# Short convolution and SwiGLU feed-forward on one core: block 2 transposed by DMA, unit 1's x loaded late and copied inside SBUF, casts in shorter rows

## The chip, the cores and the metric

The kernel runs on one core of one Trainium2 chip. The metric is the device time of one execution in microseconds. The kernel before takes 775.95 us (median of 3 runs, 775.26 to 776.23).

## The reference

The input x has 8 sequences of 4096 tokens with 192 channels in float32; the output has the same shape. The reference computes a causal convolution along the tokens and then a gated feed-forward layer:

```
w = softmax(weight, axis=-1)                     # 8 heads, 7 taps
conv[b, s, ch] = sum_k w[head(ch), k] * x[b, s - 6 + k, ch]     # 24 channels a head, zeros before the sequence
g = conv @ w_gate;  val = conv @ w_val           # 192 -> 1536
out = (g * sigmoid(g) * val) @ w_out             # 1536 -> 192
```

## The kernel before

The 32768 tokens are 64 blocks of 512 tokens, and four blocks are a unit: 16 units. The loop at L899 runs over 768 steps, 12 a block, one for each 128 columns of the hidden layer. In step n `gate_val(n)` (L771) makes six 64-row weight loads with matmuls of 64x512 (gate and val on the two halves of the array), ScalarE takes the SiLU of the gate, and VectorE multiplies it with val. Every third step a `slot` (L839) adds 24 matmuls of 64x192 of the down projection. Step 24 is the first of block 2, step 36 of block 3 and step 48 of unit 1.

For a block, `gate_val` needs the convolved tokens with the channels on the partitions: three tiles `xc[b][0..2]` of 128x512. They are made in three ways.

- Blocks 0 to 3 (unit 0) go through `early` (L373): TensorE multiplies x, loaded as overlapping windows (`xe`), with a band matrix; ScalarE and VectorE move the result into `tme`, which still has the tokens on the partitions. Blocks 0, 1 and 2 are then turned by `eturn` (L437): 15 TensorE transposes of 128x128 into three PSUM banks, and three copies on VectorE and ScalarE. Block 3 is turned by `eout` (L416), two stores of `tme` into a DRAM scratch `scre`, and `efetch` (L426), three DMA transposes from it. `early(2)` is issued inside the slot of step 12, `eturn(2)` in step 18, `early(3)` inside the slot of step 19, `eout(3)` and `efetch(3)` in steps 20 and 21.
- Units 1 and 3 go through `conv_half` (L460), which multiplies the tile `x16[u]` with the band matrix `band`: 32 matmuls each, inside the slots of steps 25 and 31 for unit 1. `x16[u]` holds the windows of x twice, in partitions 0 to 31 and 32 to 63 (and 64 to 95 and 96 to 127 for the second half of the windows). For unit 1 `load_x` (L129) reads all four pieces from DRAM, 480 KB each, before the loop starts. For unit 3 it reads two of them during unit 1, after a named SiLU, and `dup_x` (L144) copies them to the other partitions with two DMAs of 480 KB inside SBUF. The results are stored (`conv_out`, L506) and fetched by DMA transposes (`fetch`, L528).
- Units 2 and 4 to 15 are "pooled": `cast_x` (L576) casts the unit's x from DRAM into a float16 DRAM scratch `xs`, DMA transposes fetch it, and VectorE, ScalarE and GpSimd do the convolution. The cast of unit 2 is issued in step 21.

The function `seq` (L73) fixes the order of the instructions of each engine as they are written. So GpSimd's queue holds its loads and casts in program order, and SyncE (SP)'s queue holds every store, transposing fetch and copy in program order; an instruction that waits holds all that stand behind it on that engine. In the order before, SP's queue around the change is: the output of block 0 (step 17, L867), `eout(3)`, `efetch(3)`, the small fill for the cast (L583), the output of block 1, the stores of unit 1. GpSimd's is: windows `xe`, weights, `xe` again, the four loads of `x16[1]`, the four copies that build `band` (L364), the cast of unit 2 (L590).

Of the kernel before, what the change touches and what calls it, by code (L numbers as in the profile page):

```python
# [10 lines left out]
def kernel(  # L11
# [61 lines left out]
    def seq(i):  # L73

        e = i.ins.engine
        if e in last_on:
            tc.add_manual_dep(i.ins, last_on[e].name, NOSYNC, reason="order")
        last_on[e] = i.ins
        return i
# [15 lines left out]
    def windows(t, p0, t0, size, w0, w1, i0=0, i1=None, at=0, after=None):  # L95
        i1 = i1 or (Q if size == EO else size + pad)
        i = seq(
            nc.gpsimd.dma_start(  # L98
                out=t[p0 + i0 : p0 + i1, w0 - at : w1 - at, :],
                in_=bass.AP(  # L100
                    tensor=x_flat.tensor,
                    offset=(t0 + size * w0 - pad + i0) * D,
                    ap=[[D, i1 - i0], [size * D, w1 - w0], [1, D]],
                ),
            )
        )
        if after is not None:
            tc.add_manual_dep(i.ins, after.name, SYNC, reason="load in turn")
# [17 lines left out]
    def x16_tile(u):  # L126
        x16[u] = cpool.tile([P, 4 * NG, D], fp16, tag="x16", name="x16")

    def load_x(u, r, after=None, low=0):  # L129
        t, t0, w0, p0 = x16[u], u * UT, 4 * NG * r, Q * r + low  # L130
        w1 = w0 + 4 * NG
        if r == 0 and u % upb == 0:
            seq(nc.gpsimd.memset(t[0:pad, 0, :], 0.0))
            windows(t, p0, t0, CO, 0, 1, i0=pad, after=after)
            windows(t, p0, t0, CO, 1, w1)
        elif r == 1 and u == NU - 1:
            last = (UT - 1) // CO
            seq(nc.gpsimd.memset(t[p0 : p0 + 32, last - w0 :, :], 0.0))
            windows(t, p0, t0, CO, w0, last, at=w0)
            windows(t, p0, t0, CO, last, last + 1, i1=UT - CO * last + pad, at=w0)  # L140
        else:
            windows(t, p0, t0, CO, w0, w1, at=w0, after=after)

    def dup_x(u, queue=None):  # L144
        for r in range(2):
            p0 = Q * r
            seq(
                (queue or nc.sync).dma_start(
                    out=x16[u][p0 + 32 : p0 + 64], in_=x16[u][p0 : p0 + 32]
                )  # L150
            )
# [69 lines left out]
    xe_tile(3)  # L221
    xe_load(3)
    x16_tile(1)
    for r in range(2):
        for low in (0, 32):
            load_x(1, r, low=low)

    pq_i = small("pq_i", [P, 1], i32)
    seq(nc.vector.tensor_single_scalar(pq_i, pid, 15, op=ALU.bitwise_and))
# [186 lines left out]
    def eout(e):  # L416
        scre[e] = dpool.tile([XW, 4 * Q], fp16, tag="scre", name="scre")
        rows = scre[e].rearrange("(g c j) d -> c j g d", c=2, j=EO)
        for c in range(2):
            seq(  # L420
                nc.sync.dma_start(
                    out=rows[c], in_=tme[e][Q * c : Q * c + EO, :, :]
                )
            )

    def efetch(b):  # L426
        xc[b] = []
        for k in range(SL):
            t = cpool.tile([P, XW], fp16, tag=f"xc{k}", name=f"xc{k}", bufs=6)
            seq(  # L430
                nc.sync.dma_start_transpose(
                    out=t[:, 0:TB], in_=scre[b][0:TB, Q * k : Q * k + P]
                )
            )
            xc[b].append(t)

    def eturn(b, where):  # L437
        xc[b] = []
        for k in range(SL):
            t = cpool.tile([P, XW], fp16, tag=f"xc{k}", name=f"xc{k}", bufs=6)  # L440
            pool, tag = where[k]
            bank = pool.tile([P, EG, P], fp16, tag=tag, name="turn")
            for g in range(EG):
                seq(
                    nc.tensor.transpose(  # L445
                        bank[:, g, :], tme[b][:, g, Q * k : Q * k + P], ident
                    )
                )
            seq(
                (dve, act, dve)[k](  # L450
                    t.rearrange("p (g c j) -> p g c j", c=2, j=EO),
                    bank.rearrange("p g (c q) -> p g c q", c=2)[:, :, :, 0:EO],
                )
            )
            xc[b].append(t)
# [47 lines left out]
    def conv_dup(u):  # L503
        seq(nc.gpsimd.tensor_copy(tm[u][:, :, SL * Q : 4 * Q], tm[u][:, :, 0:Q]))  # L504
# [45 lines left out]
    def make_picks():  # L550
        for name in which:
            pick[name] = small(f"pick_{name}", [H, P], fp16)
            seq(
                nc.vector.scalar_tensor_tensor(
                    pick[name], which[name], float(grp), above[name],
                    op0=ALU.is_lt, op1=ALU.mult,
                )
            )
# [17 lines left out]
    def cast_x(u):  # L576
        rows = XP + UT
        xs[u] = dpool.tile([rows, D], fp16, tag="xs", name="xs")
        flat = xs[u].rearrange("t d -> (t d)")
        skip = XP if u % upb == 0 else 0  # L580
        if skip:
            seq(
                nc.sync.dma_start(  # L583
                    out=flat[0 : XP * D].rearrange("(a n) -> a n", n=P),
                    in_=fill[0 : XP * D // P, :],
                )
            )
        n = (rows - skip) * D // P
        seq(
            nc.gpsimd.dma_start(  # L590
                out=flat[skip * D : rows * D].rearrange("(a n) -> a n", n=n),
                in_=bass.AP(
                    tensor=x_flat.tensor,
                    offset=(u * UT - XP + skip) * D,
                    ap=[[n, P], [1, n]],
                ),
            )
        )
# [109 lines left out]
    def pooled(u):  # L708
        return u in POOLED
# [59 lines left out]
    silu = {}  # L769
# [117 lines left out]
    gate_bank, val_bank = (ppool, "gate"), (ppool, "val")  # L887
    acc_banks = (apool, "acc0"), (apool, "acc1")
# [10 lines left out]
    for n in range(n_steps):  # L899
        b, j = divmod(n, NCH)  # L900
        u, ls = divmod(n, ustep)
        work = None
        if n in (12, 19):

            def work(e=2 if n == 12 else 3):
                early(e, (gate_bank, gate_bank, val_bank))

        at = (25, 31) if u == 0 else (10, 22)
        if u + 1 < NU and not pooled(u + 1) and ls in at:

            def work(u=u, hh=at.index(ls)):
                conv_half(u + 1, hh)

        gate_val(n)
        if n == 6:
            early(1, (*acc_banks, gate_bank))
        elif n == 8:
            eturn(1, (*acc_banks, gate_bank))
        elif n in (9, 12, 15, 17):
            k = {9: 1, 12: 2, 15: 3, 17: 4}[n]  # L920
            slot(k, 0, silu[n - 1 if k == 4 else n - 2], work)
        elif j % 3 == 1 and n > 18:
            if j == 4 and act_steps and act_steps[0][0] < (
                dve_steps[0][0] if dve_steps else n_jobs[0]
            ) + 3:
                act_steps.pop(0)[1]()
            k = {1: 3, 4: 4, 7: 1, 10: 2}[j]
            slot(k, b - 1 if j < 7 else b, silu[n - 2], work)
        if n == 18:
            eturn(2, (*acc_banks, gate_bank))  # L930
        elif n == 20:
            eout(3)
        elif n == 21:
            efetch(3)
        if n == 34:
            make_picks()
        if n == 37:
            make_channel_taps()
        pooled_work(n, j, work is not None)
        if u + 1 < NU and not pooled(u + 1):  # L940
            if ls == at[0]:
                conv_dup(u + 1)
            if ls == at[1]:
                for m in range(2):
                    conv_out(u + 1, m)
            if ls == at[1] + 1:
                for m in range(2, 8):
                    conv_out(u + 1, m)
            lo = 32 if u == 0 else 28
            if ls in range(lo, lo + 12, 3):  # L950
                fetch(UB * (u + 1) + (ls - lo) // 3)
        if u + 2 < NU and not pooled(u + 2):
            if ls == (21 if u == 0 else 1):
                x16_tile(u + 2)
                load_x(u + 2, 0, silu[n - 1])
            if ls == (23 if u == 0 else 5):
                load_x(u + 2, 1, silu[n - 1])
            if ls == (37 if u == 0 else 26):
                dup_x(u + 2)
        for job in plan.pop(n, ()):  # L960
            job()
# [42 lines left out]
```

## Time and profile before

| | before |
|---|---|
| median of 3 runs | 775.95 us (775.26 to 776.23) |
| the profiled execution | 775.12 us, span 773.3 us |
| TensorE (PE) busy | 766.8 us, 99% |
| weight loads (PEld) / VectorE / ScalarE / GpSimd busy | 645.5 / 688.9 / 636.8 / 578.8 us |
| DMA moved | 79.32 MB, mean 103 GB/s |
| DMA queue q1 (issued from SP) | 61.58 MB, 36.3% of 16 engines |
| DMA queue q0 (issued from GpSimd) | 15.96 MB, 13.3% of 16 engines |

Times are microseconds from the start of the span of one profiled execution, which is 1.8 us shorter than that execution's own time. A row of the timeline reads: start, length, engine, line, operation, what it writes <- what it reads, shape, how many; in brackets the idle time of that engine before it and what ended that. SPq is the queue of SyncE, whose rows show how long it took to issue DMAs, not how long the data took. In the table of stages the DMA share can be over the stage's length where packets overlap.

### The profile page before, as it was taken

To read this page: it belongs to the slowest core of one execution; us is meant where nothing else is said; L and a number is where in the kernel's file an instruction comes from. 1 tells how busy PE (TensorE), PEld (TensorE's weight loads), DVE (VectorE), ACT (ScalarE), POOL (GpSimd) and SP (SyncE) were. 2 spreads that over 40 slices of the span, in tenths; PEclk is the share of its full clock that TensorE was granted. 3 is DMA by queue.
4 is the path that set the end of the run, shared out by engine and by line. 5 is a ranking of instruction groups with operands and counts; after the bars stand their busy time and mean duration, and the time that the engine had idled before them with its cause. 6 is when DMAs were issued, how large, how long until landed. Compare 5 with 4: busy or idle time off the path is not lost.

```text
span 773.3 us, 27884 instructions
## 1 busy us (share of the span) xinstructions
PE 766.8 (99%) x11179; PEld 645.5 (83%) x11179; DVE 688.9 (89%) x1034; ACT 636.8 (82%) x1093; POOL 578.8 (75%) x525
## 2 busy tenths in 40 slices
PE   8999999999999999999999999999999999999997
PEld 5666686668888888888888888888888888888886
DVE  7677998899999999999999999999999999997775
ACT  6667888888888888888888888888888888886664
POOL 8100796799989999898989989999899998882000
PEclk9999999999999999999999999999999999999999
DMA  9959855854635436355363543627454352221211
GB/s 134 190 125 135 169 118 108 158 105 101 115 96 113 107 86 106 89 118 115 77 119 84 109 101 80 123 78 122 88 111 111 87 121 74 56 70 39 67 57 42
DMA packets 143652, 79.32 MB, mean 103 GB/s; under 512 B 89146, under 2 KB 143042, under 8 KB 143042
## 3 DMA queue, kind: packets, MB, share of 16 engines
q1 hardware_dynamic: 130690, 61.58, 36.3%
q0 software_dynamic: 12832, 15.96, 13.3%
q8 instruction: 87, 1.43, 0.8%
q14 instruction: 43, 0.35, 0.2%
HBM read 31.92 MB, written 37.83 MB: 90 GB/s over the span
## 4 chain that ended last, share of the span: by engine, by line
PE 99%; ACT 0%; DVE 0%; issue 0%
PE gate L780 47%; PE acc L806 33%; PE val L780 18%; PE warm L880 0%; PE turn L445 0%; PE cv L476 0%; PE cv L387 0%; PE acc L827 0%; ACT tme L405 0%; ACT wide L345 0%; ACT o_sb L972 0%; PE taps L332 0%; DVE spread L312 0%; PE ctap L565 0%; DVE tap L310 0%
## 5 line engine op out<-in xcount | busy, mean ns | idle before, releaser
L791 DVE TENSOR_TENSOR h<-sig,val 128x512 f16<-128x512 f16 x768 | 498.8, 684 | 75.3 <-PE gate L780 51.8
L789 ACT ACTIVATE sig<-gate 128x512 f16<-128x512 f32 x768 | 458.2, 597 | 120.1 <-PE gate L780 71.8
L780 PE MATMUL gate<-pxc,w 64*128 64x512 f16 x1872 | 437.7, 376 | 0.0
L780 PE MATMUL val<-pxc,w 64*128 64x512 f16 x1872 | 437.6, 376 | 0.0
L780 PEld LDWEIGHTS <-w 64*128 64x128 f16 x4608 | 366.1, 110 | 85.2 <-issue 0.9
L806 PEld LDWEIGHTS <-h 64*128 64x128 f16 x6096 | 286.8, 94 | 29.4 <-issue 1.4
L806 PE MATMUL acc<-wo,h 64*128 64x192 f16 x6096 | 308.5, 243 | 0.0
L632 POOL TENSOR_TENSOR total<-total,part 128x512 f32<-128x512 f32 x156 | 198.3, 1271 | 64.7 <-DVE total L657 47.4
L657 DVE SCALAR_TENSOR_TENSOR total<-x,both_taps,total 128x512 f32<-128x512 f16 x156 | 166.0, 1064 | 0.0
L647 POOL TENSOR_SCALAR piece<-x,both_taps 128x512 f32<-128x512 f16 x156 | 142.9, 916 | 0.0
L632 POOL TENSOR_TENSOR total<-total,piece 128x512 f32<-128x512 f32 x78 | 111.1, 1424 | 6.5
L682 ACT ACTIVATE part<-x,both_taps 128x512 f32<-128x512 f16 x156 | 111.5, 715 | 0.0
L780 PE MATMUL val<-xc,w 64*128 64x512 f16 x432 | 102.0, 376 | 0.0
L780 PE MATMUL gate<-xc,w 64*128 64x512 f16 x432 | 101.9, 376 | 0.0
L632 POOL TENSOR_TENSOR pxc<-total,piece 128x512 f16<-128x512 f32 x52 | 66.8, 1285 | 4.3
L682 ACT ACTIVATE total<-x,both_taps 128x512 f32<-128x512 f16 x78 | 55.8, 716 | 0.0
L632 POOL TENSOR_TENSOR y<-total,piece 128x512 f16<-128x512 f32 x26 | 33.1, 1274 | 2.2
L864 DVE COPY o_sb<-acc 128x384 f32<-128x384 f32 x63 | 34.6, 549 | 0.0
L863 ACT COPY o_sb<-acc 128x384 f32<-128x384 f32 x63 | 29.8, 473 | 4.5 <-PE acc L806 4.5
L98 POOL DMA_DIRECT2D x<-in_x_dram x6 | 5.1, 871 | 24.4 <-ACT sig L789 24.4
L504 POOL COPY tm<-tm 128x1280 f16<-128x1280 f16 x2 | 2.5, 1252 | 17.3 <-DVE tm L493 17.3
L590 POOL DMA_DIRECT2D xs<-in_x_dram x13 | 7.2, 557 | 0.0
(67 smaller groups left out, 74.3 us busy)
## 6 DMA issues: line engine op xcount, KB each, us to landing
out_dram<-o_sb SPq DMA_DIRECT2D x63, 384.0 KB
pxc<-pxc SPq DMA_DIRECT2D x104, 64.0 KB
pxc<-y SPq DMA_DIRECT2D x104, 64.0 KB
xs<-in_x_dram POOLq DMA_DIRECT2D x7, 768.0 KB, 7.1
xs<-in_x_dram POOLq DMA_DIRECT2D x6, 774.0 KB, 6.8
x<-in_x_dram POOLq DMA_DIRECT2D x6, 480.0 KB, 10.1
scr<-tm SPq DMA_DIRECT2D x14, 130.0 KB
x<-x SPq DMA_DIRECT2D x26, 66.0 KB
```

The source lines that it names most:

```text
L98: nc.gpsimd.dma_start(out=t[p0 + i0 : p0 + i1, w0 - at : w1 - at, :], in_=bass.AP(tensor=x_flat.tensor, offset=(t0 + size * w0 - pad + i0) ...
L590: nc.gpsimd.dma_start(out=flat[skip * D : rows * D].rearrange("(a n) -> a n", n=n), in_=bass.AP(tensor=x_flat.tensor, offset=(u * UT - XP ...
L632: nc.gpsimd.tensor_tensor(job["dst"] if k == K - 1 else total, total, part, op=ALU.add)
L647: nc.gpsimd.tensor_scalar(part, shifted(k), scalar1=job["tap"][:, k : k + 1], scalar2=1.0, op0=ALU.mult, op1=ALU.mult,)
L657: nc.vector.scalar_tensor_tensor(job["total"], shifted(k), job["tap"][:, k : k + 1], job["total"], op0=ALU.mult, op1=ALU.add,)
L682: nc.scalar.activation(part, shifted(k), AF.Copy, scale=job["tap"][:, k : k + 1])
L780: nc.tensor.matmul(o, w16[m][p0 : p0 + Q, k, e::E], xc[b][k][p0 : p0 + Q, 0:TB], start=(k == 0), stop=(k == SL - 1),)
L789: silu[n] = seq(nc.scalar.activation(sg, g, AF.Silu)).ins
L791: seq(nc.vector.tensor_tensor(hj, sg, v, op=ALU.mult))
L806: nc.tensor.matmul(acc[b][bank][:, s, :], hj[p0 : p0 + Q, ts(2 * bank + s, P)], wo16[p0 : p0 + Q, j, :], start=(not second and j == 0 and ...
L863: seq(nc.scalar.copy(o_sb[:, 0:2, :], acc[b][0]))
L864: seq(nc.vector.tensor_copy(o_sb[:, 2:4, :], acc[b][1]))
```

## The change

Block 2 goes through `eout` and `efetch`, as block 3 does, in steps 13 and 14 in place of `eturn` in step 18. The four loads of `x16[1]` ahead of the loop are gone; two of them are issued in step 13, after the SiLU of step 12, and `dup_x(1)` in step 18 makes the other two pieces by copies inside SBUF, on SP's queue. All casts of x get a cap of 8192 bytes on a row, which is 2048 float32 elements.

```
@@ -221,9 +221,6 @@
     xe_tile(3)
     xe_load(3)
     x16_tile(1)
-    for r in range(2):
-        for low in (0, 32):
-            load_x(1, r, low=low)
 
     pq_i = small("pq_i", [P, 1], i32)
@@ -589,6 +586,7 @@
         seq(
             nc.gpsimd.dma_start(
                 out=flat[skip * D : rows * D].rearrange("(a n) -> a n", n=n),
+                max_dma_last_dim=8192,
                 in_=bass.AP(
@@ -926,8 +924,14 @@
             slot(k, b - 1 if j < 7 else b, silu[n - 2], work)
-        if n == 18:
-            eturn(2, (*acc_banks, gate_bank))
+        if n == 13:
+            eout(2)
+            for r in range(2):
+                load_x(1, r, after=silu[n - 1])
+        elif n == 14:
+            efetch(2)
+        elif n == 18:
+            dup_x(1)
         elif n == 20:
             eout(3)
```

## The prediction

> **What bounds the kernel now.** I read the page first, then the chain of waits, then the timelines of TensorE, VectorE, GpSimd and SP up to 60 us, where every edit but the cap on the casts lies.
>
> The page's first part and its chain, by engine:
>
> ```profile
> PE 766.8 (99%) x11179; PEld 645.5 (83%) x11179; DVE 688.9 (89%) x1034; ACT 636.8 (82%) x1093; POOL 578.8 (75%) x525
> PE 99%; ACT 0%; DVE 0%; issue 0%
> ```
>
> TensorE is the bound from end to end. Between 9 us and its last matmul, at 768.9, the trace has no two matmul starts more than 0.41 us apart. So work taken from TensorE's queue shortens the kernel one for one, a wait put into it lengthens it one for one, and what becomes faster elsewhere (the casts) gains nothing. The timeline of TensorE around the change:
>
> ```profile
> 28.45 0.38 PE L780 MATMUL gate<-xc,w 64*128 64x512 f16 x1
> 28.77 1.01 PE L445 MATMUL turn<-ident,tme 128*128 128x128 f16 x15
> 29.71 0.40 PE L780 MATMUL gate<-xc,w 64*128 64x512 f16 x1
> ...
> 37.20 0.66 PE L806 MATMUL acc<-wo,h 64*128 64x192 f16 x12
> 37.79 0.73 PE L476 MATMUL cv<-x,band 64*32 64x240 f16 x32
> ```
>
> The first three rows are the transposes of block 2 in step 18, the last the first use of `x16[1]` in step 25. The six gate and val matmuls of a step start in three pairs 0.215 apart; step 23's first pair stands at 35.26, so block 2 is first read, in step 24, at 35.91.
>
> Then VectorE's copy that completes `tme[2]`, GpSimd's queue and SP's queue:
>
> ```profile
> 23.33 0.26 DVE L414 COPY tme<-tme 128x320 f16<-128x320 f16 x1 [0.52 <-DVE tme L405]
> ```
> ```profile
> 17.40 3.42 POOL L98 DMA_DIRECT2D x<-in_x_dram  x4
> 20.78 1.76 POOL L364 COPY band<-wide 32x256 f16<-32x256 f16 x4
> 22.50 0.54 POOL L590 DMA_DIRECT2D xs<-in_x_dram  x1
> ```
> ```profile
> 28.90 0.42 SPq L867 DMA_DIRECT2D out_dram<-o_sb  x1
> 32.98 2.50 SPq L421 DMA_DIRECT2D scre<-tme  x2
> 39.08 3.83 SPq L431 DMA_TRANSPOSE xc<-scre  x3
> ```
>
> The four loads of x are issued by 20.82, and the last has landed 15.6 later, at 35.5: only 2.3 us before its first reader. Block 3's store needs 6.1 us from its first issue (32.98) until SP may issue the transposes (39.08).
>
> **What the change removes: about 1.0 us.** Without `eturn(2)`, step 19 starts one pair spacing after the pair at 28.45, at 28.67 instead of 29.71: 1.04 us. Its three evictions leave engines that wait for TensorE there, and count nothing. The two loads and the earlier DMA traffic that go away were hidden before (no stall), so they count nothing either.
>
> **What it adds: two new deadlines.** Block 2 must be in place by 35.91 - 1.04 = 34.9, and all four pieces of `x16[1]` by 37.79 - 1.04 = 36.75. Each microsecond by which the later piece misses is lost. I follow SP's queue in its new order: store of block 2, its transposes, output of block 0, two copies, store of block 3.
>
> Store: it can start when the copy at 23.33 ends, 23.6. Until its landing I have 6.1 us (block 3's, beside a cast) above; below, the stores of unit 1, issued each 0.65 us after the last with landing marks 2.1 us after issue, give 2.5. Now two x loads run beside it, so I take 5.0: 28.6.
>
> Transposes: issued in 3.83 as block 3's were: 32.4. The last lands 1.4 (undisturbed) to 2.7 after: 34 to 35, about at the deadline. A stall here is covered by the larger one below.
>
> x loads: the SiLU of step 12 starts them at 21.6, issued 0.9 apart. The nearest rows are unit 3's two loads, the first alone and the second beside transposes:
>
> ```profile
> x<-in_x_dram POOLq DMA_DIRECT2D x1, 480.0 KB, 7.6
> x<-in_x_dram POOLq DMA_DIRECT2D x1, 480.0 KB, 9.9
> ```
>
> So they land at about 29.2 and 32.4, before SP is ready to copy. Ahead of the copies stands also the output of block 0, 0.42 to issue: 32.8. The cast of unit 2 now follows the loads on GpSimd at 23.4, 0.9 later than before; its own reader waits until step 36, so that costs nothing.
>
> Copies: unit 3's are the only row, behind two outputs:
>
> ```profile
> 86.47 2.14 SPq L867 DMA_DIRECT2D out_dram<-o_sb  x2
> 88.70 1.88 SPq L148 DMA_DIRECT2D x<-x  x2
> ```
>
> The last landing mark of the second copy stands at 97.1, 8.4 after 88.70; the packets themselves run from 91.2 to 94.9. From 32.8 this gives 41.2. Below: with nothing ahead in the ring some 6 us, 38.8. Above: the cast of unit 2 is then in flight. What a cast does to SP's DMAs is seen at 143.7, where one (8.5 us to landing) runs beside eight transposes, which undisturbed take 1.25 each to issue:
>
> ```profile
> 141.85 14.83 SPq L534 DMA_TRANSPOSE xc<-scr  x8
> ```
>
> That is 4.8 us lost to one cast, whose packets (24,576 bytes, some 2 us each in the trace) alternate with short ones. Shorter rows should let SP's packets through oftener, so I add 1 us of the possible 0 to 4.8: 42.3.
>
> **The sum.** The convolution half starts at 42.3 instead of 37.79: +4.5, which already holds the -1.04. Everything behind it shifts alike. The store of block 3 comes out of SP's queue near 35 and lands behind the copies, near 43; its transposes end near 48, while step 36 is then past 50, so this adds nothing. Its cover gone, it would cost at most what the copies cost. The profiled execution, 775.12, becomes 779.6; it stands 0.83 below the median of 775.95, so the median becomes 780.4. Ends of the unknowns: store 2.5 to 6.1, copies 6 to 8.4, cast 0 to 4.8, which gives 36.3 to 47.2, net -1.04 (nothing stalls) to +9.4.
>
> **A rule against the trace.** Unit 3's loads of 480 KB took 7.6 and 9.9 us to land. The Trainium skill, "DMA: Bandwidth & Descriptors", section "Anatomy of one DMA", has a fit of 2.0 us plus the bytes over 436 GB/s, which makes such a load 3.1 us. An estimate of the whole chain by it (store 2.6, both copies 4.3) ends near 36, in time, and the median would be 774.9; the rows of this case are two to three times longer, so I keep them.
>
> A second rule speaks against the change. After the last matmul at 768.9, the granted clock in the table of stages falls to a mean of 0.75 in the last 1.2 us, after some 3.7 us of idleness. "TensorE: Matmul & The Clock Gate", section "Part 1: The HAM clock gate", says that an idle window of about 3.4 us halves the clock until some 3.4 us of work have passed. An estimate by it adds 1.7 us where one stall is that long.
>
> **The rivals.**
>
> 1. *SP's DMAs are not held and all arrive in time, or nearly.* Store 2.5, transposes 3.83 and no disturbance put the copies at 30.3, and 6 us later is 36.3, before 36.75. Then only the 1.04 is left: 774.9. For it: TensorE's own gain is certain, and the initial backlog of loads is gone by 21.6. Against: the output issued at 28.90 beside the x loads has no packet in the trace until 32.5. Anything up to 39.3 ends within 0.2% of before, which is 1.55 us and about what a measurement of this kernel can tell from no change. Chance 0.22. This is the side that is not slower; the deciding point is a landing of the second copy before 36.75.
> 2. *The store of block 2 is held until the loads and the cast are through.* They are queued back to back on GpSimd, 480 + 480 KB at the 190 GB/s of the stages at 24 to 30 us (5.2 us) and the cast (some 5 us): from 24 to 34 or 35. Then transposes end near 39, block 2 stalls step 24 by 5 us, and the copies land near 47: +9, about 785, and a lower clock could come on top. For it: the silent output at 28.90. Against: transposes at 66 to 68 us went through beside an x load, slowly. Chance 0.13.
> 3. *The cap does not change the packets,* or changes them without helping SP. Then the hold of the cast is up to 4.8 instead of my 1: +8.3 at most, within the range. It decides only where a cast meets a copy or a transpose that TensorE awaits, which happens once, near 32 to 38 us.
>
> A gain beyond 1.55 us has no row: TensorE has no other gap to close. I leave 0.03 for what I do not see.
>
> **How the numbers follow.** Late copies, net +1.6 to +8, 0.62; held store, 0.13; in time or nearly, 0.22; a larger gain, 0.03. So faster 0.03, same 0.22, slower 0.75. The late-copies case alone runs from 777.5 to 784; the range takes in the case of no stall, 774.9, and the lower part of the held store, up to 785.
>
> **What would show it.** Right: no `turn` row at 28.8; step 19 about 1 us earlier; an idle gap of TensorE of some 4 to 6 us in all between 34.9 and 43, most of it before the first `cv<-x,band` row of line 476, released by a DMA of `x<-x`; the copies issued at 32 to 35 on SP; from step 31 on the same spacing as before, shifted. Cast packets near 4 KB. Wrong: matmuls running through step 25 without a gap; or the larger gap at step 24, before the first matmul that reads block 2, which would mean that store and transposes, and not the copies, set the loss; or any gap after 60 us, which I have not priced.

## The result and the profile after

The changed kernel takes 786.56 us (median of 5 runs, 786.03 to 788.72), the kernel before beside it 775.87: 1.0145 times as long (95% interval 1.0134 to 1.0156), 10.7 us more. The profiled execution took 786.03, its span 783.8, against 775.12 and 773.3.

The page of the changed kernel, busy times and the chain by engine:

```profile
PE 769.4 (98%) x11164; PEld 681.7 (87%) x11164; DVE 688.5 (88%) x1032; ACT 635.3 (81%) x1092; POOL 577.3 (74%) x523
PE 96%; DMA 2%; SPq 1%; ACT 0%; issue 0%; DVE 0%
```

TensorE has 15 matmuls fewer, the transposes, and yet the chain that ended last now runs for 3% through transfers and through SP's queue, where 99% of it was TensorE before. The waits of TensorE between 30 and 60 us (what waited, for what: us in total, times, longest) and its timeline there:

```profile
PE gate L778 <- DMA xc<-scre: 4.9, 3, 3.2
PE cv L473 <- DMA x<-x: 3.4, 2, 2.0
```
```profile
34.85 0.38 PE L778 MATMUL gate<-xc,w 64*128 64x512 f16 x1
...
38.46 0.40 PE L778 MATMUL gate<-xc,w 64*128 64x512 f16 x1 [3.22 <-DMA xc<-scre]
...
39.94 0.42 PE L778 MATMUL gate<-xc,w 64*128 64x512 f16 x1 [1.08 <-DMA xc<-scre]
...
41.06 0.58 PE L778 MATMUL gate<-xc,w 64*128 64x512 f16 x1 [0.63 <-DMA xc<-scre]
...
45.18 0.26 PE L473 MATMUL cv<-x,band 64*32 64x240 f16 x1 [1.37 <-DMA x<-x]
47.44 1.00 PE L473 MATMUL cv<-x,band 64*32 64x240 f16 x31 [2.00 <-DMA x<-x]
```

Step 24 waits three times, once for each of block 2's transposes, and step 25 twice, once for each copy. SP's queue shows why all five are late:

```profile
24.14 1.19 SPq L418 DMA_DIRECT2D scre<-tme  x2
35.87 3.83 SPq L428 DMA_TRANSPOSE xc<-scre  x3
39.80 0.54 SPq L865 DMA_DIRECT2D out_dram<-o_sb  x1
40.39 1.27 SPq L148 DMA_DIRECT2D x<-x  x2
```

The store of block 2 is issued at 24.14, and SP may go on only at 35.87: 11.7 us. The two x loads (issued 22.28 and 23.15) have landed by 28.8 and 32.2 and the cast (24.00) by 36.0, by their landing marks, the semaphore updates that the trace records for a transfer (up to 16). The DMA view of the stage from 24 to 28 us, in which both halves of the store are issued (24.14 and 24.55), has no packet of q1, SP's queue:

```profile
q0 software_dynamic: 1493, 0.57, 131.4%
...
xs<-in_x_dram POOLq DMA_DIRECT2D x1, 768.0 KB, 12.0
x<-in_x_dram POOLq DMA_DIRECT2D x1, 480.0 KB, 9.1
scre<-tme SPq DMA_DIRECT2D x2, 130.0 KB
```

The store's first data packet comes at 28.2, 4.0 us after its issue. From there on its packets of 512 bytes alternate with those of the second load and then with the cast's of 4096 bytes, which take 0.32 us each; one landing mark after another comes in until 35.8.

A third loss stands in the table of stages (stage, then busy time and instructions of each engine, granted clock, DMA share, GB/s):

```profile
40.10:43.50 3.40, 2.77 (x20) 1.47 (x19) 0.69 (x1) 1.14 (x2) 0.00 (x0) 0.51 1.18 285
43.50:47.00 3.50, 0.57 (x7) 0.14 (x3) 0.69 (x1) 0.06 (x1) 0.00 (x0) 0.99 0.69 175
47.00:50.40 3.40, 2.96 (x49) 1.89 (x51) 1.22 (x2) 1.02 (x2) 0.90 (x1) 0.50 0.37 86
```

After each of the two stretches of waiting the clock is halved for 3.4 us. The first time this costs nothing, since the copies are awaited afterwards anyway. The second time it delays real work.

Following the first matmul of a step in both traces gives the whole account, as after minus before: step 18 +0.42 (this execution started that much later), step 19 -0.62, step 20 -0.84, step 24 +2.55, step 25 +4.89, step 26 +10.35, step 28 +10.89, and from there to step 767 it stays at +10.88. So the missing transposes won 1.26 by step 20, and the waits and the clock took 11.72 behind it. Nothing behind 51 us is won or lost.

### The profile page after: what moved, and what is told of

It is laid out like the page before. It is cut to its first block, busy times and chain, and to the rows that moved or that the text cites. A ratio compares the mean times of both kernels' runs of the same rounds, so it can differ in the third digit from the quotient of the medians.

```text
span 783.8 us, 27860 instructions
## 1 busy us (share of the span) xinstructions
PE 769.4 (98%) x11164; PEld 681.7 (87%) x11164; DVE 688.5 (88%) x1032; ACT 635.3 (81%) x1092; POOL 577.3 (74%) x523
## 4 chain that ended last, share of the span: by engine, by line
PE 96%; DMA 2%; SPq 1%; ACT 0%; issue 0%; DVE 0%
PE gate L778 38%; PE acc L804 31%; PE val L778 26%; DMA scre<-tme 1%; DMA x<-x 1%; PE warm L878 1%; SPq L428 0%; PE cv L473 0%; PE acc L825 0%; PE turn L442 0%; PE cv L384 0%; ACT tme L402 0%; SPq L148 0%; ACT wide L342 0%; ACT sig L787 0%
## 5 line engine op out<-in xcount | busy, mean ns | idle before, releaser
L778 PEld LDWEIGHTS <-w 64*128 64x128 f16 x4608 | 400.1, 110 | 64.1 <-issue 4.4
L804 PEld LDWEIGHTS <-h 64*128 64x128 f16 x6096 | 296.5, 94 | 22.2 <-issue 1.5
L804 PE MATMUL acc<-wo,h 64*128 64x192 f16 x6096 | 315.2, 243 | 0.0
L778 PE MATMUL gate<-xc,w 64*128 64x512 f16 x432 | 103.6, 380 | 5.0 <-DMA xc<-scre 4.9
L778 PE MATMUL val<-xc,w 64*128 64x512 f16 x432 | 103.8, 380 | 0.0
L630 POOL TENSOR_TENSOR y<-total,piece 128x512 f16<-128x512 f32 x26 | 33.1, 1274 | 2.2
L98 POOL DMA_DIRECT2D x<-in_x_dram x4 | 3.4, 857 | 29.2 <-ACT sig L787 29.2
L490 ACT CAST tm<-cv 128x480 f16<-128x480 f32 x8 | 4.1, 562 | 5.4 <-PE cv L473 5.4
```

The source lines that it names most:

```text
L490: eng(tm[u][:, NG * r : NG * r + NG, 2 * grp * hp : 2 * grp * hp + 2 * grp].rearrange("p g (t e) -> p g t e", t=2), banks[r][:, 0 : 2 * w] ...
L630: nc.gpsimd.tensor_tensor(job["dst"] if k == K - 1 else total, total, part, op=ALU.add)
L778: nc.tensor.matmul(o, w16[m][p0 : p0 + Q, k, e::E], xc[b][k][p0 : p0 + Q, 0:TB], start=(k == 0), stop=(k == SL - 1),)
L804: nc.tensor.matmul(acc[b][bank][:, s, :], hj[p0 : p0 + Q, ts(2 * bank + s, P)], wo16[p0 : p0 + Q, j, :], start=(not second and j == 0 and ...
```

## The experiments

Theory A: whatever SP issues while GpSimd's loads or cast have data in flight is held until these are nearly through; two transfers that TensorE needs (block 2, then the copies) queue up behind that one hold. Rivals: B, the store is slow by itself; C, only the loads hold, not the cast; D, only the loads of step 13 do the harm.

**The cast of unit 2 later** (changed kernel):

```
-            cast, jobs = 21, 55
+            cast, jobs = 30, 55      # and: the cast waits for the SiLU of its step
```

> The changed kernel, with the cast of unit 2 asked for in step 30 instead of 21, after the SiLU of that step; all else as changed. Theory A (SP's store of block 2 is held as long as GpSimd's queue has data in flight, loads and cast alike): the second store lands soon after the second x load (32.2 in the changed kernel), at 32.5 to 33.5 instead of 35.8; the transposes are issued near 33 instead of 35.87, the copies land near 44.4 instead of 47.3, and the median falls by some 3 us, to about 783.5. Rival B (the store is slow by itself, its 512-byte rows take some 11 us to DRAM): nothing moves, 786.5. Rival C (only the x loads hold it, the cast in short rows lets it through): nothing moves either, the second store still lands near 35.8.

Measured: 783.19, 7.7 over the kernel before (ratio 1.0099, 1.0084 to 1.0114). SP's queue:

```profile
24.36 1.10 SPq L418 DMA_DIRECT2D scre<-tme  x2
33.12 3.82 SPq L428 DMA_TRANSPOSE xc<-scre  x3
```

The store now takes 8.8 us instead of 11.7, and its last mark, 33.1, follows 15 of the 16 marks of the second load (by 32.6; the last stands at 34.3). So the cast made some 3 us of the hold. C falls.

**Without the cap** (changed kernel less the line `max_dma_last_dim=8192`):

> The changed kernel without the cap on the casts' rows (packets of 24,576 bytes again). Theory A: the hold lasts as long as the cast's data, whose sum of bytes is the same; the second store lands with the end of the cast, at 36 to 38 instead of 35.8, so the median is 786.5 to 789. If shorter rows let SP's packets through in earnest, the store now lands more than 3 us later and the median is over 789.5. Rival B: no change, 786.5.

Measured: 787.05 (ratio 1.0154, 1.0138 to 1.0170), and SP's transposes are issued at 35.82. With the cap the packets of the cast are 4096 bytes, without it 24,576; the hold is the same. The cap does what it says, but helps neither SP's queue here nor, alone (below), anything else.

**The x loads later** (changed kernel; loads from step 13 to step 18, cast to step 30, so that GpSimd's queue is silent while block 2 is turned):

```
-            for r in range(2):
-                load_x(1, r, after=silu[n - 1])
...
         elif n == 18:
+            for r in range(2):
+                load_x(1, r, after=silu[n])
+        elif n == 19:
             dup_x(1)
```

> The changed kernel with the two x loads asked for in step 18 after its SiLU, the copies queued behind the output of block 0 as before, and the cast in step 30, so that GpSimd's queue is silent while block 2 is stored and transposed. Theory A: the second store lands within 3.5 us of its first issue, by 27.7; the transposes are issued from there and block 2 is in place before 34.9, so that step 24 starts without a stall (the row that waits for xc<-scre disappears). The x loads then land near 36 and 38.5, the copies near 45 to 47, and one stall before the first convolution half takes all the loss: 784 to 788. Rival B: the store lands at 35 or later as in the changed kernel and step 24 stalls as there.

Measured: 784.98 (ratio 1.0129, 1.0112 to 1.0146). SP's queue and all that TensorE waited for from 30 to 60 us:

```profile
23.59 1.04 SPq L418 DMA_DIRECT2D scre<-tme  x2
26.42 3.85 SPq L428 DMA_TRANSPOSE xc<-scre  x3
```
```profile
PE cv L473 <- DMA x<-x: 8.9, 2, 6.4
```

This is the decisive run. The same store needs 2.8 us, a quarter of 11.7, block 2's last mark stands at 33.4, and step 24 does not wait. B falls. The output of block 0, issued at 30.37 beside the new place of the loads, is now the one that is held: its landing marks come from 38 to 40. The copies land at 45.7, so TensorE waits for them alone.

**The three parts alone** (each put into the kernel before):

> The kernel before with the cap on the casts' rows alone. TensorE waits for none of SP's transfers after 60 us in either kernel: no change, within 0.2% of before. If some wait of TensorE hid in the casts, it would be faster by over 0.2%.

> The kernel before with block 2 turned by store and transposes in steps 13 and 14, alone; the four x loads stand ahead of the loop and the cast in step 21 as before. Theory A (held): GpSimd's queue has data in flight from 17 to 39 us, so the store issued at 23.6 lands at 36 to 39, block 2 is in place at 41 to 44 and step 24 stalls by 6 to 9 us: 781 to 785, more with a halved clock. Rival D (only the loads asked for in step 13 do the harm, by meeting the store): the store lands near 28.6, block 2 by 34.9, and the removed 1.04 us shows: 774.5.

> The kernel before with the two late x loads of step 13 and the copies of step 18, alone; block 2 is turned on TensorE in step 18 as before, the casts have no cap. Theory A: the second load lands near 32.2, the copies are issued then, behind the output of block 0, which the loads and the cast hold until some 36; the copies land at 40 to 42 instead of the 37.8 at which they are needed: net +2 to +5, 778 to 781. If the copies alone made the loss of the whole change, 786; if they are hidden, 775.5.

The cap alone: 775.30 (ratio 0.9996, 0.9987 to 1.0005), no change. Block 2 alone: 781.20 (1.0075, 1.0061 to 1.0088), +5.5. The late loads and copies alone: 777.40 (1.0024, 1.0015 to 1.0033), +1.7. The sum of the parts is 7.1, the whole 10.7. SP's queue with block 2 alone, then with the late x alone:

```profile
24.30 0.81 SPq L421 DMA_DIRECT2D scre<-tme  x2
31.90 7.71 SPq L431 DMA_TRANSPOSE xc<-scre  x3
```
```profile
28.90 0.42 SPq L864 DMA_DIRECT2D out_dram<-o_sb  x1
29.38 5.13 SPq L148 DMA_DIRECT2D x<-x  x2
```

What TensorE waited for from 30 to 60 us with block 2 alone:

```profile
PE gate L780 <- DMA xc<-scre: 4.8, 3, 3.6
```

With the four old loads in flight the store takes 7.6 us and the transposes 7.7 to issue instead of 3.83: block 2 is late although no load stands in step 13, so D falls too. I had expected the store to be held to 36 or later; it landed at 31.9, and the rest of the delay fell on the transposes. The late x alone costs little because SP is free for the copies at 29.4, where in the whole change it stands until 40.39 behind block 2. That queueing is what the two parts do to each other.

**The clock** (changed kernel, dummy matmuls on zeros put into TensorE's queue where it waits):

```
+        if n == 24:
+            rewarm(14)
         gate_val(n)
...
+                if u == 0 and hh == 0:
+                    rewarm(12)       # in the second of these runs 10
                 conv_half(u + 1, hh)
```

> The changed kernel with 14 dummy matmuls of 512 columns on TensorE's queue before step 24 and 12 before the first convolution half (3.0 and 2.6 us at full clock), which fit into the two stalls. If the halved clock after the stalls (40.1 to 43.6 and 47.0 to 50.4 in the changed kernel) is part of the loss, the granted clock stays at 1.0 from 7 us to the end, the copies land at the same time, and the work after 47 us runs at full rate: 1.0 to 1.8 us less, about 785.0. If the clock costs nothing: 786.5, or up to 788 should the dummies outlast the stalls.

The first run gave 785.36, but without the changed kernel beside it; so both went once more, together:

> The changed kernel once more, beside the next two on one chip, as their yardstick: 786 to 787.

> The changed kernel with 14 dummy matmuls before step 24 and 10 before the first convolution half. Theory A with the clock: the clock is at 1.0 again when the last copy lands, so the 3.4 us of half clock behind it, worth 1.7 us, are gone; the dummies cost nothing, for they end before the copies land: 1.0 to 1.8 us less than the changed kernel beside it. Rival: the loss is the wait alone, no difference over 0.3 us.

Measured: 787.71 for the changed kernel (a little over the 786 to 787 expected), 785.18 with the dummies: 2.5 us less, more than the 1.8 expected. The stage behind the last copy, first in the repeated changed kernel, then with dummies:

```profile
48.00:52.00 4.00, 4.00 (x55) 2.15 (x57) 1.26 (x3) 1.62 (x3) 1.25 (x1) 0.50 0.23 41
```
```profile
47.60:51.00 3.40, 3.40 (x73) 2.26 (x75) 2.15 (x4) 2.48 (x5) 1.25 (x1) 1.00 0.23 52
```

The dummies did not keep the clock up throughout: it still halved from 41.2 to 44.6, where that hides behind the wait. It was whole again when the copies landed. How much the clock takes differs between executions: in the trace of the repeated changed kernel it stood at half from 38.46 to 52.11 without a break, in the first one from 40.14 to 43.55 and from 46.97 to 50.38, and the medians were 787.71 and 786.56. Against the lower of the two the dummies won 1.2 (785.36) and 1.4 (785.18).

**Three versions meant to keep the gain.** All have the convolution halves in steps 31 and 34, with fetches three steps later, and block 2 by transposes.

```
-        at = (25, 31) if u == 0 else (10, 22)
+        at = (31, 34) if u == 0 else (10, 22)
-            lo = 32 if u == 0 else 28
+            lo = 35 if u == 0 else 28
```

First, both x loads ahead of the loop and the cast in step 30. In the kernel that ran, the copies stand in step 18 behind the output of block 0, not directly behind the transposes as its expectation says.

> A version that keeps TensorE's 1.04 us and gives the transfers room: block 2 by store and transposes in steps 13 and 14, the two x loads ahead of the loop and not in step 13, the copies on SP directly behind the transposes of block 2, the convolution halves of unit 1 in the slots of steps 31 and 34 instead of 25 and 31 with their fetches three steps later, and the cast of unit 2 in step 30. Theory A: GpSimd's queue is empty near 28, the store lands near 30, block 2 near 35, about at its need (34.9 to 35.3); the copies land near 40, before their need at 42.8; 774.5 to 776, faster than before by up to 0.13%. Rival B or an unseen wait: a stall at step 24 of over 2 us, 777 or more.

Measured: 778.07 (ratio 1.0024, 1.0015 to 1.0033). Step 24 still waits 0.4 us, and the cast, issued at 43.36, meets block 3's transposes, issued from 43.24: step 36, where there was no wait before, waits 2.3 us. Both waits together, from 30 to 75 us:

```profile
PE gate L784 <- DMA xc<-scre: 2.7, 4, 1.4
```

Second, one load ahead of the loop, one in step 18, the cast in four parts (each `128 / 4` rows) in steps 26, 30, 35 and 38:

> A version made from what the runs showed: one x load ahead of the loop, the other in step 18 after the SiLU of step 17, when block 2's transposes are nearly through; the copies in step 18 behind the output of block 0; the convolution halves in the slots of steps 31 and 34, their fetches three steps later; the cast of unit 2 in four parts in steps 26, 30, 35 and 38, each after its step's SiLU. Theory A: GpSimd's queue is empty from about 25 to 31, the store lands near 27, block 2 near 33 (needed at 34.9), the copies near 41 (needed at 42.8), block 3 before 48; no stall of TensorE over 0.5 us, and the 1.04 us of the transposes show: ratio to before 0.998 to 0.9995. Rival: one of these transfers is held by a part of the cast and TensorE stalls by 1 us or more: ratio 1.0005 or more.

Measured: 778.50, spread from 775.37 to 781.63 (ratio 1.0036, 1.0023 to 1.0048). The second load, issued at 28.54, still met the transposes issued at 28.80; so step 24 waits 1.2 us. Step 48 waits 1.7 us for block 4 (`scr`):

```profile
PE gate L803 <- DMA xc<-scr: 1.7, 1, 1.7
PE gate L803 <- DMA xc<-scre: 1.2, 1, 1.2
```

Block 4's stores ran beside a part of the cast that landed at 59.0, and the packets of its third transpose then paused for about a microsecond near 62.5, with no packet of GpSimd's queue after 58.7, for a reason that the trace does not show.

Third, the second load in step 20, its copy behind block 3's store, the four parts in steps 30 to 33:

> The version with one early load, with its two stalls taken away by order: the second x load in step 20 after the SiLU of step 19, two microseconds later, so that it can't meet block 2's transposes; its copy behind block 3's store; the four parts of the cast in steps 30 to 33, ahead of unit 1's stores and fetches. Theory A: block 2 near 33.5 (needed at 34.9), the second copy near 43 (needed at 42.8, so up to 0.5 us late), block 4 before 61; ratio to before 0.9985 to 1.0005. Rival: a part of the cast still holds a transfer that TensorE awaits and a stall of over 1 us stands in the profile: ratio 1.0010 or more.

Measured: 778.76, spread from 776.44 to 782.85 (ratio 1.0043, 1.0025 to 1.0061). GpSimd's load, SP's transposes and TensorE's waits to 75 us:

```profile
30.58 0.87 POOL L98 DMA_DIRECT2D x<-in_x_dram  x1 [10.27 <-ACT sig L812]
```
```profile
28.01 4.24 SPq L429 DMA_TRANSPOSE xc<-scre  x3
```
```profile
PE gate L803 <- DMA xc<-scre: 3.0, 1, 3.0
PE gate L803 <- DMA xc<-scr: 1.1, 1, 1.1
```

The third transpose was issued at 30.60, 0.02 us after the load; its packets ran from 33.5 to 36.7, for most of the time in alternation with the load's, and it landed at 38.3, the load at 38.1. In the first and the third version the clock halved as well (from 52.81 to 56.22, from 39.46 to 42.87), so their traces lose more than the waits. In all three the ratio came out on the rival's side. The transfers awaited at steps 36 and 48, or the stores ahead of them, ran beside the cast; at step 24, though, the second and the third version waited beside the x load, which their rivals had not named. No version beat the kernel before, and I did not find a place for all of these transfers. What stays open is whether one exists: it could win at most the 1.26 us that the transposes cost.

## Why the prediction was wrong

The direction was right and the mechanism was one of the rivals; the size was off by more than half. Of its steps:

- *The transposes removed from TensorE, 1.04.* Right for the step itself: from step 18 to step 19 the difference between the traces goes from +0.42 to -0.62. But the three evictions, which the prediction counted as nothing, cost 0.22 more: by step 20 the difference is -0.84. `eturn(2)` writes two of its tiles into the banks of `acc`, which the slot of step 19 needs, and before the change the weight loads of that slot pause from 30.28 to 30.58, until VectorE's first copy out of these banks (from 30.10) is over. So the change removed 1.26. That the copy made the pause fits the rows and was not tested by itself.
- *The store of block 2, taken as 5.0 with bounds of 2.5 and 6.1.* This is the step that failed. It measured 11.7. The lower bound was true to the row (2.8 with GpSimd's queue silent), the upper was not: block 3's store, my row for "beside a cast", was issued at 32.98 and had its first packet at 35.6, when all but one of the data packets of GpSimd's queue had started (by 35.2), so it showed the end of a hold and not a whole one. The better row was at hand and quoted against a rival: the output issued at 28.90 beside the x loads, with no packet until 32.7 and its last landing mark at 39.9, 11 us after its issue. The DMA view of the kernel before from 29 to 32.4 us has packets of q0 and none of q1:

```profile
q0 software_dynamic: 1237, 0.78, 167.6%
out_dram<-o_sb SPq DMA_DIRECT2D x1, 384.0 KB
```

  A second row was misread. Unit 3's first load (62.95), called alone in the prediction, had a transpose beside it that was issued at 63.21 and landed at 70.5, with the load; block 3's first transpose, issued at 39.08, landed 2.6 us later. The rival of the held store, at 0.13, had the mechanism and nearly the size (+9), and two of its places: 5 us at step 24 (measured 4.9) and copies near 47 (47.3).
- *The transposes, 3.83 to issue.* Right, 3.83.
- *The x loads at 29.2 and 32.4.* Right, 28.8 and 32.2.
- *The copies, 8.4 and 1 for the cast, 42.3.* Over: 6.9 from their issue (40.39 to 47.3). The cast was over by then, and one output stood ahead of them, where the row had two. This took back part of the store's error by luck: they were issued 7.6 later than forecast (40.39, not 32.8) and landed 5.0 later.
- *The place of the loss.* I put most of it before the first convolution half. TensorE waited 4.9 us at step 24 and 3.4 at step 25, the case that the prediction named as its refutation.
- *The clock*, left out of the sum. From the convolution to step 28 the kernel before takes 2.46 us (37.79 to 40.25), the changed one 3.70 from the end of its last wait (the second matmul of the convolution, 47.44, to 51.14): 1.2. In the repeated pair it was 2.5 by the medians. The prediction's estimate by the Trainium skill, "TensorE: Matmul & The Clock Gate", section "Part 1: The HAM clock gate", was 1.7, between the two; the skill's window of about 3.4 us agrees with the 3.413 us of half clock in the trace.
- *Block 3 and the rest hidden, the cap without effect on TensorE.* Right.
- *The estimate of the whole chain by a fit, near 36.* The terms that it names (23.6, store 2.6, transposes 3.83, output 0.42, copies 4.3) add up to 34.8. Both are in time, so the forecast does not change; the copies landed at 47.3.

By the landing of the copies, the 10.88 of the steady state divide into two: the convolution goes on at 47.44 and not at 37.79, +9.65; half a clock behind it, +1.2. This is read from the same two traces and is no second proof.

## What to carry to other kernels

The time of a transfer is not a property of the transfer: the same store of 2 x 130 KB took 2.8 us with the other queue silent and 11.7 beside it, so a row is a fair price only if what else was in flight, from its issue on, is the same. When work moves from a busy engine to DMA, list what each queue has in flight between the new issue and the new need, and then everything that stands behind the waiting instruction on its own queue: here the wait for a store also held the copies that TensorE needed next. Cutting long rows into shorter packets, with the same bytes in flight, did not shorten the hold here (SP went on at 35.87 with the cap and at 35.82 without).

## What the runs showed of the hardware

- *A transfer of SP's queue that comes after a load of GpSimd's has begun can get nothing for some time, then every other packet.* In the changed kernel there is no packet of it from 24.14 to 28.2, in the kernel before none from 28.90 to 32.7, in the run with later loads none of the output issued at 30.37 until 35.5. With GpSimd's queue silent the first packet came after 0.9 and 1.1 us (the store of the run with later loads, 23.59 to 24.4; the output of the changed kernel, 39.80 to 40.9). The silence is not always so long: in the first of the three versions the store issued at 23.99, with the second load still in flight, began at 25.6. The turns show best in the third version, with 231 packets of SP's transpose and 236 of the load from 34.5 to 35.5. The Trainium skill, "DMA: Bandwidth & Descriptors", section "Queues, rings and completion order", says that an engine goes round its queues by packets; the alternation agrees with that, the silence of 3.8 to 5.2 us before it is not explained there, and no run here settles its cause.
- *It is enough to be issued at about the same time:* the transpose issued 0.02 us after a load landed with it, 7.7 us later, where an undisturbed one lands some 2.5 us after its issue (35.87 to 38.4 in the changed kernel).
- *A halved clock can follow a wait that is broken up:* the clock fell at 40.1 in the changed kernel, with two matmuls at 38.46 and two at 39.94 in the stretch from 35.2 on, and at 52.8 in the first of the three versions behind waits of 0.87 and 1.42. In all fourteen traces the clock changes only at multiples of 3.413 us from its first rise. Taken by these stretches, it halved after those with at most 1.38 us of busy TensorE (0.60 in the changed kernel from 36.73; 1.38 in the run with 12 dummies from 39.56) and stayed whole after 1.49 and 1.55 (from 35.03 in the run with later loads, from 37.56 in the one with the later cast). Once halved, it came back after 2.78 (changed kernel, from 40.14) and not after 2.52 (the repeated one, from 41.87), which fits how long the repeated one stayed at half.
